# A cross network on one core: how the first block's chunk 2, tails and biases get to their places

## The chip, the core and the metric

The kernel runs on one core of a Trainium2 chip. The core has TensorE (PE; matmuls into PSUM, which has eight banks), VectorE (DVE), ScalarE (ACT), GpSimd (POOL), SyncE (SP, which here only issues DMAs), and 16 DMA engines that move data between HBM and SBUF. DMAs are issued on two queues here, SP's and ACT's. The metric is the device time of one execution in microseconds (us).

## The reference

```python
B, F, D, L = 4096, 26, 16, 6          # rows of 416 values, bfloat16
def reference(x0, ws, bs):            # x0 [4096, 416], ws [6, 416, 416], bs [6, 416]
    x = x0
    for l in range(ws.shape[0]):
        x = x0 * (x @ ws[l] + bs[l]) + x
    return x
```

## The kernel before, in words

The kernel never forms x. It keeps the sums x0 ws[0] + ... in PSUM: after layer l, PSUM holds the sum over layers of x @ ws, DVE adds a running sum of biases (plus one, from the ones row of `bsa_sb` and the triangle `u_sb`) and multiplies by x0. That gives the next x.

*Tiling.* The 4096 rows are worked in four pairs (p) of two blocks of 512 rows. Everything is transposed: features lie on partitions, rows of x0 in the free dimension. The 416 features are three chunks of 128 and a **tail** of 32. The tails of a pair are packed: four groups of 32 partitions hold the tails of the four quarters of 256 rows. A tail matmul therefore needs the 32 tail rows of the weights four times, at partitions 0, 32, 64 and 96 (`w3_sb`), and the tail-to-tail corner as a block diagonal 128 x 128 (`wc_sb`).

*Order on TensorE, written by hand.* For each of the 24 steps n = 6p + l: `main` for block 0 (helper `columns`, L398, L378), `tail` (L464: tail features into the chunks; then corners, L398; then chunks into the tail, L485), `main` for block 1. Step 0 is different: `first` (L345 on) takes the place of block 0's `main`.

*The start.* `idle` (L304) runs 28 matmuls of ones. SP's queue carries: half of x0's first 512 rows (`xin_sb`, 416 columns, L159), three chunks of ws[0] (L163), block 1 of x0 transposed by DMA (L166, three chunks), then, after the last chunk of ws[0] has landed, the weights of layers 1 to 5 (L171) each with its four tail copies (`four`, L174), and then the other pairs. ACT's queue carries the other half of `xin_sb` (L607), the tails of block 1 (`xtb_sb`, L610), the biases (`bsa_sb`, L613) and one copy of the tail weights of ws[0] (`w30_sb`, L614).

`first` turns the 512 rows on TensorE: 12 transposes (`turn`, L316), whose results DVE copies out in four pieces (L557). Then `biases` (L332, L338: three matmuls of 128 columns, and four of 32 into the four tail groups). Then, for each input chunk k of layer 0, four matmuls (helper `whole`, L388). After k = 0 come two transposes of the packed tails (L359), and `four_tails`: one matmul of `rep_sb` (four identities side by side) with `w30_sb`, which makes the four copies of the tail weights in PSUM.

DVE, after its four copies, takes the biases out (`cb_sb`, L562), then the tails (L567), and swaps halves of them (L570, semaphore s_dup). ACT takes the four tail copies out (L630) into `w3_sb`, then it and POOL copy two corners each into `wc_sb` (L623, L272). POOL packs the tails before that (L262), from `xin_sb` and `xtb_sb`. The first `tail` waits for the tails (s_ev, s_dup), the biases (s_cb), the weights (s_w30), and within it for the corners (s_wc0, s_wc) and for block 1 of x0 (s_x0[0]).

Of the kernel before, what the change touches and what calls it, by code (L numbers as in the profile page):

```python
# [11 lines left out]
def bass_standalone__dcn_v2_cross__recsys_kernel(  # L12
# [13 lines left out]
    B, D = x0.shape  # L26
# [13 lines left out]
    with ExitStack() as es:  # L40
# [7 lines left out]
        w30_sb = sb("w30_sb", [DR, D])  # L48
        rep_sb = sb("rep_sb", [DR, 128])
# [4 lines left out]
        xin_sb = sb("xin_sb", [128, 4, D])  # L54
        xtb_sb = sb("xtb_sb", [128, 4, DR])
# [13 lines left out]
        bsa_sb = sb("bsa_sb", [L + 1, D])  # L69
        u_sb = sb("u_sb", [L + 1, L])  # L70
# [22 lines left out]
        def blocks(l):  # L93

            gs = [slice(32 * g, 32 * g + 32) for g in range(4)]
            return [(wc_sb[g, l, g], w3_sb[g, l, DF:D]) for g in gs]
# [13 lines left out]
        s_bs, s_cb, s_wc = sem("s_bs"), sem("s_cb"), sem("s_wc")  # L110
        s_wt = [sem("s_wt%d" % i) for i in range(L)]
# [45 lines left out]
        def _(sp):  # L157

            sp.dma_start(  # L159
                xin_sb[:, 0:2, :], x0[0:256, :].rearrange("(j b) d -> b j d", b=128)  # L160
            ).then_inc(s_xin[0], 16)
            for k in range(3):
                sp.dma_start(  # L163
                    w_sb[:, 0, k, :], ws[0, k * 128:(k + 1) * 128, :]
                ).then_inc(s_w0[k], 16)
            sp.dma_start_transpose(  # L166
# [72 lines left out]
        def _(pool):  # L239
# [11 lines left out]
            pool.affine_select(  # L251
                out=rep_sb[:, :].rearrange("f (g e) -> f g e", e=DR),
                in_=ones_sb[0:DR, :].rearrange("f (g e) -> f g e", e=DR),
                pattern=[[0, 4], [-1, DR]], compare_op=ALU.is_equal, fill=0.0, base=0,
                channel_multiplier=1,
            ).then_inc(s_setup, 1)
            pool.memset(wc_sb[:, :, :], 0.0).then_inc(s_g, 1)

            for h, src in enumerate((xin_sb[:, :, DF:D], xtb_sb[:, :, :])):
                for x in (s_xin, (s_xtb,))[h]:  # L260
                    pool.wait_ge(x, 16)
                pool.tensor_copy(  # L262
                    out=xtn_sb[:, 0, :, :].rearrange(
                        "b c (h k f) -> b c h k f", h=2, f=DR
                    )[:, :, :, h, :],
                    in_=src.rearrange("b (h c) f -> b c h f", c=2),
                ).then_inc(s_xtp, 1)
            pool.wait_ge(s_xtp, 2)
            pool.wait_ge(s_g, 1)
            pool.wait_ge(s_w30, 1)  # L270
            for o, i in blocks(0)[2:]:
                pool.tensor_copy(out=o, in_=i).then_inc(s_wc0, 1)  # L272
            pool.wait_ge(s_wc0, 2)
# [25 lines left out]
        def _(pe):  # L299
# [6 lines left out]
            idle(28)  # L306
            pe.wait_ge(s_setup, 4)
            def at(c, j):

                return 4 if (c, j // 2) == (0, 1) else (2, 3, 6)[c]  # L310
# [13 lines left out]
            def four_tails():  # L324

                pe.wait_ge(s_wt[0], 16)
                whole(ps[:, 3, 0:D], rep_sb[:, :], w30_sb[:, :], True, True).then_inc(s_inT, 1)

            def biases():
                pe.wait_ge(s_bs, 16)  # L330
                for c in range(3):
                    pe.matmul(  # L332
                        ps[:, 7, D + c * 8:D + c * 8 + L],
                        lhsT=bsa_sb[:, c * 128:(c + 1) * 128], rhs=u_sb[:, :],
                        start=True, stop=True,
                    )
                for g in range(4):
                    ins = pe.matmul(  # L338
                        ps[32 * g:32 * g + 32, 7, D + 24:D + 24 + L],
                        lhsT=bsa_sb[:, DF:D], rhs=u_sb[:, :],  # L340
                        start=True, stop=True, tile_position=(0, 32 * g),
                    )
                ins.then_inc(s_inT, 1)

            def first():  # L345

                for c in range(3):
                    turn(c)
                biases()
                for k in range(3):  # L350
                    pe.wait_ge(s_w0[k], 16)
                    pe.wait_ge(s_ev, k + 2)
                    for m in range(3):
                        for o, x in pieces(0, m, xsrc(0, 0, 0, k)):
                            whole(o, w_sb[:, 0, k, m * 128:(m + 1) * 128], x, k == 0, False)
                    if k == 0:
                        pe.wait_ge(s_xtp, 2)
                        for c in range(2):
                            ins = pe.transpose(  # L359
                                out=psT[:, 2, c * 128:(c + 1) * 128],  # L360
                                in_=xtn_sb[:, 0, c, :], identity=ident[:, :],
                            )
                        ins.then_inc(s_inT, 1)
                        pe.wait_ge(s_ev, 3)
                        four_tails()
# [79 lines left out]
            def tail(p, l, n):  # L445
                if n == 0:
                    pe.wait_ge(s_ev, 5)
                    pe.wait_ge(s_cb, 1)
                    pe.wait_ge(s_w30, 1)
                elif l == 0:  # L450
                    pe.wait_ge(s_x0t[p], 16)
                elif n < L:
                    pe.wait_ge(s_wt[l], 16)
# [21 lines left out]
                if n == 0:  # L475
                    pe.wait_ge(s_wc0, 2)
                if n < L:
                    pe.wait_ge(s_wc, 4 * n + 2)
# [75 lines left out]
        def _(dve):  # L554
            for i, (c, j0, j1) in enumerate(((0, 0, 2), (0, 2, 4), (1, 0, 4), (2, 0, 4))):
# [3 lines left out]
                    in_=psT[:, (2, 4, 3, 6)[i], j0 * 128:j1 * 128],  # L559
                ).then_inc(s_ev, 1)  # L560
            dve.wait_ge(s_inT, 5)
# [4 lines left out]
            dve.wait_ge(s_inT, 6)  # L566
            dve.tensor_copy(out=x0t_sb[:, 0, 0, :], in_=psT[:, 2, 0:NT]).then_inc(s_ev, 1)  # L567
            dve.wait_ge(s_ev, 5)
            for o, i in swapped(x0t_sb[:, 0]):
                dve.tensor_copy(out=o, in_=i).then_inc(s_dup, 1)  # L570
# [35 lines left out]
        def _(act):  # L606
            act.dma_start(  # L607
                xin_sb[:, 2:4, :], x0[256:512, :].rearrange("(j b) d -> b j d", b=128)
            ).then_inc(s_xin[1], 16)
            act.dma_start(  # L610
                xtb_sb[:, :, :], x0[NB:2 * NB, DF:D].rearrange("(j b) d -> b j d", b=128)
            ).then_inc(s_xtb, 16)
            act.dma_start(bsa_sb[1:L + 1, :], bs[:, :]).then_inc(s_bs, 16)  # L613
            act.dma_start(w30_sb[:, :], ws[0, DF:D, :]).then_inc(s_wt[0], 16)  # L614
# [4 lines left out]
            def corner(l):  # L619
                if l > 0:  # L620
                    act.wait_ge(s_wt[l], 16)
                for o, i in blocks(l)[:2 if l == 0 else 4]:
                    act.activation(out=o, in_=i, func=ACTF.Copy).then_inc(s_wc, 1)  # L623

            def other(ap):
# [3 lines left out]
            act.wait_ge(s_inT, 7)  # L629
            act.activation(  # L630
                out=w3_sb[:, 0, :], in_=ps[:, 3, 0:D], func=ACTF.Copy
            ).then_inc(s_w30, 1)
            act.wait_ge(s_g, 1)
            act.wait_ge(s_w30, 1)
            corner(0)
# [79 lines left out]
```

## Time and profile before

| what | value |
| --- | --- |
| time, median of 3 runs | 129.96 us (129.71 to 130.29) |
| the profiled execution: time | 130.26 us |
| its span, first to last instruction | 128.5 us |
| TensorE busy | 124.4 us, 97% |
| DVE, ACT, POOL busy | 92.3, 45.9, 32.0 us |
| chain of waits that ended last | TensorE 97% |

The profile comes from one execution. A page of it gives the busy time of each engine, the chain of waits that ended last, groups of instructions by line (mean ns of one, idle time before them and what ended it), and DMA issues. Times within the span are counted from its start. "L388" is line 388 of the kernel before; helpers such as `whole` and `columns` carry the line for all that call them. A start of a matmul and the end of the one before it overlap, since they are pipelined. In the chain a piece begins where the piece before it ended. A DMA's "us to landing" is counted from the start of its issue.

### The profile page before, as it was taken

Reading aid. Unit: us, or ns where it says so; the run is one execution under the profiler, and the core shown is the slowest. Engines: PE = TensorE matmul, PEld = TensorE weight load, DVE = VectorE, ACT = ScalarE, POOL = GpSimd, SP = SyncE. Lnnn points to the kernel's source line nnn. Section 1 sums busy time; section 2 is a strip of 40 time slices with the busy share of each in tenths; the row PEclk is TensorE's granted clock in tenths of the full one; section 3 lists DMA queues with packets and bytes.
Section 4 is the critical chain, followed back from the end, with each engine's and each line's share of the span. In section 5 each row is a group of like instructions: output and inputs, shape, how many; then the busy total and the mean of one; then the engine's idle time right before and its main releaser. Section 6 shows DMA issues by size and latency. Waiting matters only on the chain.

```text
span 128.5 us, 5801 instructions
## 1 busy us (share of the span) xinstructions
PE 124.4 (97%) x2929; PEld 66.2 (52%) x2402; DVE 92.3 (72%) x152; ACT 45.9 (36%) x101; POOL 32.0 (25%) x40
## 2 busy tenths in 40 slices
PE   7999999999999999999999999999999999999990
PEld 7654554555445545545545545545545545546660
DVE  0439669669669669669679678688687697696482
ACT  1345446436404314314404224224214224225920
POOL 6123303303303203213113123123023033033050
PEclk9999999999999999999999999999999999999999
DMA  3979659665969940496300968000000857000026
GB/s 107 267 196 246 171 118 112 123 66 113 116 197 163 122 88 15 85 145 181 114 15 10 133 122 265 5 0 5 5 10 15 161 122 233 5 5 0 0 67 203
DMA packets 35463, 13.27 MB, mean 103 GB/s; under 512 B 26826, under 2 KB 35440, under 8 KB 35440
## 3 DMA queue, kind: packets, MB, share of 16 engines
q1 hardware_dynamic: 34436, 12.52, 48.7%
q10 hardware_dynamic: 1004, 0.38, 1.1%
q8 instruction: 21, 0.34, 1.1%
q14 instruction: 2, 0.02, 0.0%
HBM read 3.99 MB, written 3.41 MB: 58 GB/s over the span
## 4 chain that ended last, share of the span: by engine, by line
PE 97%; DVE 0%; issue 0%
PE ps L398 61%; PE ps L378 11%; PE ps L464 8%; PE ps L388 7%; PE ps L485 6%; PE ps L304 2%; PE ps L316 1%; DVE o_sb L600 0%; PE ps L528 0%; PE ps L332 0%; PE ps L338 0%; PE ps L359 0%
## 5 line engine op out<-in xcount | busy, mean ns | idle before, releaser
L579 DVE SCALAR_TENSOR_TENSOR xT_sb<-ps,cb_sb,x0T_sb 128x512 bf16<-128x512 f32 x100 | 69.3, 743 | 22.5 <-PE ps L464 22.5
L398 PE MATMUL ps<-xT_sb,w_sb 128*32 128x512 bf16 (+1 forms) x1380 | 75.7, 343 | 0.0
L398 PEld LDWEIGHTS ps<-xT_sb,w_sb 128*32 128x32 bf16 x1380 | 37.1, 97 | 35.0 <-issue 8.1
L285 POOL TENSOR_TENSOR xT_sb<-t_sb,x0T_sb 128x512 bf16<-128x512 f32 x20 | 23.3, 1163 | 72.0 <-ACT t_sb L661 72.0
L661 ACT ACTIVATE t_sb<-ps,cb_sb 128x512 f32<-128x512 f32 x23 | 15.8, 687 | 60.0 <-PE ps L464 60.0
L378 PE MATMUL ps<-xT_sb,w_sb 128*32 128x256 bf16 x444 | 26.6, 273 | 0.0
L627 ACT ACTIVATE xt_sb<-xt_sb 64x256 bf16<-64x256 bf16 x38 | 15.8, 415 | 9.8 <-DVE xt_sb L588 9.3
L398 PE MATMUL ps<-x0T_sb,w_sb 128*32 128x512 bf16 (+1 forms) x252 | 14.1, 344 | 0.0
L579 DVE SCALAR_TENSOR_TENSOR xo_sb<-ps,cb_sb,x0T_sb 128x512 bf16<-128x512 f32 x15 | 10.4, 743 | 3.3 <-PE ps L464 3.3
L398 PEld LDWEIGHTS ps<-x0T_sb,w_sb 128*32 128x32 bf16 x252 | 6.7, 97 | 6.5 <-issue 1.5
L464 PE MATMUL ps<-xt_sb,w_sb 32*128 32x256 bf16 x228 | 9.6, 271 | 0.0
L485 PE MATMUL ps<-xT_sb,w_sb 128*32 128x256 bf16 x228 | 9.5, 273 | 0.0
L588 DVE SCALAR_TENSOR_TENSOR xt_sb<-ps,cb_sb,x0t_sb 128x256 bf16<-128x256 f32 x20 | 9.5, 475 | 0.0
L464 PEld LDWEIGHTS ps<-xt_sb,w_sb 32*128 32x128 bf16 x228 | 4.2, 92 | 6.2 <-issue 6.1
L285 POOL TENSOR_TENSOR xo_sb<-t_sb,x0T_sb 128x512 bf16<-128x512 f32 x3 | 3.5, 1164 | 11.2 <-ACT t_sb L661 11.2
L485 PEld LDWEIGHTS ps<-xT_sb,w_sb 128*32 128x32 bf16 x228 | 6.1, 96 | 0.1
L398 PE MATMUL ps<-xt_sb,wc_sb 128*32 128x256 bf16 x76 | 5.6, 283 | 0.0
L623 ACT ACTIVATE wc_sb<-w_sb 32x32 bf16<-32x32 bf16 x22 | 5.0, 227 | 0.6
L388 PE MATMUL ps<-w_sb,xT_sb 128*128 128x416 bf16 x24 | 5.0, 339 | 0.0
L378 PE MATMUL ps<-x0T_sb,w_sb 128*32 128x256 bf16 x84 | 5.0, 273 | 0.0
L600 DVE SCALAR_TENSOR_TENSOR o_sb<-ps,xr_sb 128x416 bf16<-128x416 f32 x6 | 3.3, 585 | 2.4 <-PE ps L528 2.3
L557 DVE COPY x0T_sb<-ps 128x256 bf16<-128x256 bf16 (+1 forms) x4 | 1.4, 358 | 4.5 <-PE ps L316 4.3
(54 smaller groups left out, 48.3 us busy)
## 6 DMA issues: line engine op xcount, KB each, us to landing
out_dram<-o_sb SPq DMA_DIRECT2D x3, 832.0 KB, 4.9
w_sb<-in_ws_dram SPq DMA_DIRECT2D x5, 312.0 KB, 5.5
w_sb<-in_ws_dram SPq DMA_DIRECT2D x8, 104.0 KB, 3.4
xr_sb<-in_x_dram SPq DMA_DIRECT2D x1, 832.0 KB, 6.4
out_dram<-o_sb SPq DMA_DIRECT2D x3, 208.0 KB, 2.1
xin_sb<-in_x_dram SPq DMA_DIRECT2D x1, 208.0 KB, 3.0
xin_sb<-in_x_dram ACTq DMA_DIRECT2D x1, 208.0 KB, 3.3
x0T_sb<-in_x_dram SPq DMA_TRANSPOSE x13, 4.2
```

The lines of the kernel that those rows point to most:

```text
L285: pool.tensor_tensor(out=xdst(p, l, 0, 2), in0=t_sb[:, n % 2, :], in1=x0c(p, 0, 2), op=ALU.mult,).then_inc(s_pl, 1)
L378: return pe.add_instruction(mybir.InstMatmult(name="I-%d" % (1000000 + count[0]), engine=mybir.EngineType.PE, start_tensor_calc=start, sto ...
L388: return pe.matmul(out, lhsT=lhsT, rhs=rhs, start=start, stop=stop, skip_group_check=True)
L398: ins = pe.matmul(out[c:c + 32, :], lhsT=lhsT[:, c:c + 32], rhs=rhs, start=start, stop=stop, skip_group_check=True, tile_position=(0, c),)
L464: ins = pe.matmul(part(blk, m, h ^ other), lhsT=w3_sb[32 * g:32 * g + 32, l, m * 128:(m + 1) * 128], rhs=xt[32 * g:32 * g + 32, other, :], ...
L485: ins = pe.matmul(ps_tail[32 * g:32 * g + 32, :], lhsT=w_sb[:, l, k, DF:D], rhs=xsrc(p, l, g % 2, k)[:, (g // 2) * NT:(g // 2 + 1) * NT], ...
L579: dve.scalar_tensor_tensor(out=halves(xdst(p, l, blk, c)), in0=chunk2(blk, c), scalar=cb_sb[:, c, l:l + 1], in1=halves(x0c(p, blk, c)), op ...
L588: dve.scalar_tensor_tensor(out=tdst(p, l), in0=ps_tail, scalar=cb_sb[:, 3, l:l + 1], in1=x0t_sb[:, p, 0, :], op0=ALU.add, op1=ALU.mult,).t ...
L600: dve.scalar_tensor_tensor(out=o_sb[:, (NP - 1) * TT + j, :], in0=ps[:, BANK[j], 0:D], scalar=1.0, in1=xr_sb[:, j, :], op0=ALU.add, op1=AL ...
L623: act.activation(out=o, in_=i, func=ACTF.Copy).then_inc(s_wc, 1)
L627: act.activation(out=o, in_=i, func=ACTF.Copy).then_inc(s_dup, 1)
L661: act.activation(out=halves(t_sb[:, n % 2, :]), in_=chunk2(0, 2), func=ACTF.Identity, bias=cb_sb[:, 2, l:l + 1],).then_inc(s_act, 1)
```

## The change

Block 0's chunk 2 is no longer turned on TensorE: `xin_sb` holds 256 columns, and a DMA transpose on SP's queue, ahead of that of block 1, brings chunk 2. The third chunk of ws[0] moves to ACT's queue. The tails of both blocks come in one load (`xtb_sb`, 1024 rows of 32 values) on ACT's queue. The tail weights of ws[0] come as two copies in one load (`two`) straight into the lower half of `w3_sb`, and ACT copies that half to the upper; `four_tails`, `rep_sb` and `w30_sb` are gone. The four corners of layer 0 are all copied by POOL, one after the other, straight from the loaded rows. The biases are issued last on ACT's queue; POOL makes four copies of their tail part (`bs4_sb`), so that four equal matmuls make the sums; those stand after k = 1 now. The last chunk, k = 2, waits for the DMA transpose in place of a DVE copy. There are 27 idle matmuls. DVE takes the biases out after the tails.

```diff
-        w30_sb = sb("w30_sb", [DR, D])
-        rep_sb = sb("rep_sb", [DR, 128])
...
-        xin_sb = sb("xin_sb", [128, 4, D])
-        xtb_sb = sb("xtb_sb", [128, 4, DR])
+        xin_sb = sb("xin_sb", [128, 4, 256])
+        xtb_sb = sb("xtb_sb", [128, TT, DR])
...
+        bs4_sb = sb("bs4_sb", [L + 1, 4, DR])
...
+        def two(l):
+            return ws[l, DF:D, :].unsqueeze(0).broadcast_to([2, DR, D])
...
         def _(sp):
             sp.dma_start(
-                xin_sb[:, 0:2, :], x0[0:256, :].rearrange("(j b) d -> b j d", b=128)
+                xin_sb[:, 0:2, :], x0[0:256, 0:256].rearrange("(j b) d -> b j d", b=128)
             ).then_inc(s_xin[0], 16)
-            for k in range(3):
+            for k in range(2):
                 sp.dma_start(
                     w_sb[:, 0, k, :], ws[0, k * 128:(k + 1) * 128, :]
                 ).then_inc(s_w0[k], 16)
+            sp.dma_start_transpose(
+                out=x0T_sb[:, 2, 0:NB], in_=x0[0:NB, 256:DF]
+            ).then_inc(s_xa2, 16)
             sp.dma_start_transpose(
                 out=x0T_sb[:, :, NB:2 * NB], in_=x0[NB:2 * NB, 0:DF]
             ).then_inc(s_x0[0], 16)
...
         def _(pool):
...
-            for h, src in enumerate((xin_sb[:, :, DF:D], xtb_sb[:, :, :])):
-                for x in (s_xin, (s_xtb,))[h]:
-                    pool.wait_ge(x, 16)
+            pool.wait_ge(s_xtb, 16)
+            for k in range(2):
                 pool.tensor_copy(
...
-            pool.wait_ge(s_w30, 1)
-            for o, i in blocks(0)[2:]:
-                pool.tensor_copy(out=o, in_=i).then_inc(s_wc0, 1)
-            pool.wait_ge(s_wc0, 2)
+            pool.wait_ge(s_bs, 16)
+            pool.wait_ge(s_setup, 1)
+            pool.tensor_copy(
+                out=bs4_sb[:, :, :], in_=bsa_sb[:, DF:D].unsqueeze(1).broadcast_to([L + 1, 4, DR])
+            ).then_inc(s_bs4, 1)
+            pool.wait_ge(s_g, 1)
+            pool.wait_ge(s_wt[0], 16)
+            for g in range(4):
+                gs = slice(32 * g, 32 * g + 32)
+                pool.tensor_copy(out=wc_sb[gs, 0, gs], in_=w3_sb[0:DR, 0, DF:D]).then_inc(s_wc0, 1)
+                pool.wait_ge(s_wc0, g + 1)
...
         def _(pe):
-            idle(28)
-            pe.wait_ge(s_setup, 4)
+            idle(27)
+            pe.wait_ge(s_setup, 3)
...
-            def four_tails():
-
-                pe.wait_ge(s_wt[0], 16)
-                whole(ps[:, 3, 0:D], rep_sb[:, :], w30_sb[:, :], True, True).then_inc(s_inT, 1)
-
             def biases():
-                pe.wait_ge(s_bs, 16)
-                for c in range(3):
-                    pe.matmul(
+                pe.wait_ge(s_bs4, 1)
+                for c in range(4):
+                    ins = pe.matmul(
                         ps[:, 7, D + c * 8:D + c * 8 + L],
-                        lhsT=bsa_sb[:, c * 128:(c + 1) * 128], rhs=u_sb[:, :],
-                        start=True, stop=True,
-                    )
-                for g in range(4):
-                    ins = pe.matmul(
-                        ps[32 * g:32 * g + 32, 7, D + 24:D + 24 + L],
-                        lhsT=bsa_sb[:, DF:D], rhs=u_sb[:, :],
-                        start=True, stop=True, tile_position=(0, 32 * g),
+                        lhsT=bsa_sb[:, c * 128:(c + 1) * 128] if c < 3
+                        else bs4_sb[:, :, :].rearrange("l g f -> l (g f)"),
+                        rhs=u_sb[:, :], start=True, stop=True,
                     )
                 ins.then_inc(s_inT, 1)
 
             def first():
 
-                for c in range(3):
+                for c in range(2):
                     turn(c)
-                biases()
                 for k in range(3):
                     pe.wait_ge(s_w0[k], 16)
-                    pe.wait_ge(s_ev, k + 2)
+                    if k < 2:
+                        pe.wait_ge(s_ev, k + 2)
+                    else:
+                        pe.wait_ge(s_xa2, 16)
...
                         ins.then_inc(s_inT, 1)
-                        pe.wait_ge(s_ev, 3)
-                        four_tails()
+                    elif k == 1:
+                        biases()
...
                 if n == 0:
-                    pe.wait_ge(s_ev, 5)
+                    pe.wait_ge(s_ev, 4)
                     pe.wait_ge(s_cb, 1)
                     pe.wait_ge(s_w30, 1)
+                    pe.wait_ge(s_wt[0], 16)
...
         def _(act):
             act.dma_start(
-                xin_sb[:, 2:4, :], x0[256:512, :].rearrange("(j b) d -> b j d", b=128)
+                xin_sb[:, 2:4, :], x0[256:512, 0:256].rearrange("(j b) d -> b j d", b=128)
             ).then_inc(s_xin[1], 16)
             act.dma_start(
-                xtb_sb[:, :, :], x0[NB:2 * NB, DF:D].rearrange("(j b) d -> b j d", b=128)
+                xtb_sb[:, :, :], x0[0:2 * NB, DF:D].rearrange("(j b) d -> b j d", b=128)
             ).then_inc(s_xtb, 16)
+            act.dma_start(w_sb[:, 0, 2, :], ws[0, 256:DF, :]).then_inc(s_w0[2], 16)
+            act.dma_start(w3_sb[0:64, 0, :], two(0)).then_inc(s_wt[0], 16)
             act.dma_start(bsa_sb[1:L + 1, :], bs[:, :]).then_inc(s_bs, 16)
-            act.dma_start(w30_sb[:, :], ws[0, DF:D, :]).then_inc(s_wt[0], 16)
...
-            act.wait_ge(s_inT, 7)
+            act.wait_ge(s_wt[0], 16)
             act.activation(
-                out=w3_sb[:, 0, :], in_=ps[:, 3, 0:D], func=ACTF.Copy
+                out=w3_sb[64:128, 0, :], in_=w3_sb[0:64, 0, :], func=ACTF.Copy
             ).then_inc(s_w30, 1)
-            act.wait_ge(s_g, 1)
-            act.wait_ge(s_w30, 1)
-            corner(0)
```

## The prediction

> **What bounds the kernel now.** I read the page first. TensorE is busy nearly the whole span and the chain that ended last is made of it:
>
> ```profile
> PE 124.4 (97%) x2929; PEld 66.2 (52%) x2402; DVE 92.3 (72%) x152; ACT 45.9 (36%) x101; POOL 32.0 (25%) x40
> ...
> PE 97%; DVE 0%; issue 0%
> ```
>
> So from the first tail matmul of layer 0 (L464) on, TensorE waits for nothing. The change touches only what comes before that point; later work can absorb no delay and return no gain. The question is when that first L464 matmul starts. The chain of waits over the first microseconds (start, length, what) says when it does now:
>
> ```profile
> 3.97 1.40 PE ps L316 x12
> 5.37 0.17 PE ps L332 x3
> 5.54 0.12 PE ps L338 x2
> 5.66 1.13 PE ps L388 x4
> 6.79 0.11 PE ps L359 x2
> 6.90 0.28 PE ps L388
> 7.18 0.16 issue
> 7.34 1.25 PE ps L388 x7
> 8.59 0.44 PE ps L464 x12
> ```
>
> The tail starts at **8.59**. Note the speed: four matmuls (1536 columns) take 1.13 us at 5.66, and twice that takes 1.25 at 7.34; twelve turns take 1.40, but two take 0.11 at 6.79. TensorE runs at half speed until about 6.4. Third, the stretches by window (last two columns: DMA busy share, GB/s):
>
> ```profile
> 2.00:6.00 4.00, 4.00 (x40) 3.23 (x38) 1.44 (x5) 1.49 (x2) 1.37 (x4) 1.00 1.11 278
> 6.00:6.50 0.50, 0.50 (x3) 0.23 (x2) 0.00 (x0) 0.00 (x0) 0.00 (x0) 1.00 0.72 155
> 5.50:6.00 0.50, 0.50 (x8) 0.21 (x7) 0.42 (x2) 0.00 (x0) 0.00 (x0) 1.00 1.27 289
> 7.75:8.00 0.25, 0.25 (x4) 0.12 (x3) 0.00 (x0) 0.17 (x1) 0.11 (x1) 1.00 1.09 369
> 8.25:8.50 0.25, 0.25 (x3) 0.05 (x1) 0.00 (x0) 0.06 (x1) 0.16 (x2) 1.00 0.86 77
> 8.50:8.75 0.25, 0.25 (x10) 0.22 (x12) 0.00 (x0) 0.00 (x0) 0.18 (x1) 1.00 0.76 70
> 26.50:27.00 0.50, 0.50 (x16) 0.28 (x12) 0.50 (x2) 0.26 (x2) 0.00 (x0) 1.00 0.31 29
> ```
>
> The DMA engines are full from 2.0 to about 6.3. From 7.75 to 8.00 a plain layer load flows (832-byte rows, 369 GB/s). Then, although the layer-2 load was issued at 6.96, the rate falls to 70 to 77: what flows is the tail load of layer 1 (`four`, L174), four copies of 32 rows. An engine moving such rows does 369/16 = 23 GB/s, so it uses about three to four of the 16, and holds back what is queued behind it.
>
> **TensorE's own work.** One idle matmul less is 0.11, but now the first turn also waits for x0's rows until 3.8 (issue 0.79 + 3.0 to landing). They shrink from 416 to 256 columns, so I let the turns start at 3.75: 0.2 gained. Eight turns instead of twelve end at 4.65 (0.107 each). The first layer matmuls wait for the second DVE copy: 4.86 now, at best 4.75 then. k=0 at half speed: 1.28 (twice the 0.64 of a full-speed one), to 6.05; two tail turns, 0.22, to 6.27; k=1 0.7, to **7.0**. The `rep_sb` matmul and the gap behind it (0.28 + 0.16) are gone. Then come the biases, four matmuls, 0.2, and k=2, 0.64. With nothing late the tail would start at 7.8, a gain of 0.77.
>
> **What must be there by then.**
> - *Chunk 2 by DMA.* Issued at 2.27. Its issue is bounded by 1.24 (the L189 transpose) and 1.58 (L166, three chunks). Its 131 KB take 0.45 at 289 GB/s, up to 0.9 shared, and 0.5 more to landing: about 5.3, at most 6.5 (by the 4.2 of L166). Wanted at 7.2 or later: nothing, hidden by k=0 and k=1. Copying chunk 2 on DVE (0.42) goes and nothing waited for it.
> - *Small tails.* 1024 pieces of 64 bytes instead of 512: 65 KB at 29/0.31 = 94 GB/s, 0.70 instead of 0.35, landing about 4.9; two POOL copies (0.29 each) end at 5.5, wanted at 6.05. Nothing.
> - *x0 block 1* (L166) is pushed behind chunk 2: issue 3.55 to 5.14, needed in the tail's third part, 0.66 after the tail starts. See below.
> - *Layer 1 and later weights.* SP is free at 5.14 instead of 5.76, and w0's third chunk now comes on ACT's queue; they are issued at 5.2 to 5.6 and needed at 11.4. Nothing.
> - *Setup and queues.* The select that made `rep_sb` (0.30 on POOL, done at 2.1) goes; the first turn is at 3.75: nothing. ACT issues five loads instead of four, so its table load ends near 5 instead of 4.2; ACT's next work waits for the tail weights: nothing. DVE's bias copy is moved behind the three tail copies, which end at 7.4; it waits for the biases anyway.
> - *Tail weights and biases* are what I think decides. The load `two` is of the same kind as `four`: two copies of 32 rows of 832 bytes. The biases (6 rows) are moved **behind** it on ACT's queue, and the bias matmuls now stand **ahead of k=2**, so TensorE's queue stops there until the biases land and POOL has copied four tails of them.
>
> **When they land.** In full-rate terms all DMA ahead of `two` on its engines is: x0 262 KB, 0.85 (between 0.71 at 369 and the present 1.15); w0 0.87; small tails 0.70; chunk 2 0.45: 2.87. The present load sums to 1.15 + 0.87 + 0.35 + 0.09 + 1.36 = 3.82 the same way and took 4.3, so I scale by 1.13: `two` starts at 4.9 to 5.25. If it runs on two engines it takes 53 KB at 46 GB/s, 1.15, or 1.4 to 1.5 at half of the 70 to 77 seen. Block 1's transposes (1.36) are ready at 5.14 on the other queue. Alone `two` ends at 6.1 to 6.4; shared evenly, at 7.2 to 7.8. Even sharing is what the trace shows: the two halves of x0, issued within 0.01 on two queues, landed 3.0 and 3.3 after issue. With 0.5 to landing (the transposes' share falls at 6.4, L166 lands at 2.75 + 4.2), weights and biases are there at T = 6.6 to 8.3. I take **T = 7.7**, near the shared end.
>
> The Trainium skill, page DMA: Bandwidth & Descriptors, section "Rules for kernel authors", says that the slowest dimension sets the number of DMA engines and that "a leading zero-stride broadcast of c copies — confines the whole DMA to at most c engines". The rate of the four-copy load agrees (70 to 77 of 369 GB/s). It speaks against this change: by it `two` has two engines; were it spread over 16, it would cost 0.15.
>
> **From T to the tail.** POOL starts 0.05 after the landing (small tails: 1.31 + 3.4 = 4.71, copy at 4.73). The bias copy, 7 x 128, is in no row: between 0.18 (L247, 7 x 6) and 0.29 (L262, 128 x 128); I take 0.25. To TensorE 0.15 (the gap at 7.18), biases 0.2, k=2 0.64: tail at T + 1.29, so **break-even is T = 7.3**. With 7.7 it starts at 8.99: **+0.40**. TensorE idles from 7.0 to about 8.15. The other inputs of the tail fit beside this: ACT's copy of 64 x 416, bounded by the rows below, ends at T + 0.7; DVE's bias copy (0.17) at T + 0.95; POOL's four corners, now one after the other, 0.24 to 0.35 each, I take 0.28, end at T + 1.5, wanted at T + 1.73. Block 1 on the loaded engines: 2.0 + 1.13 (2.87 + 1.15 + 1.36) = 8.1, landing 8.6, wanted at 9.6.
>
> ```profile
> 7.22 0.52 ACT L630 ACTIVATE w_sb<-ps 128x416 bf16<-128x416 f32 x1 [2.83 <-PE ps L388]
> 7.83 0.48 ACT L623 ACTIVATE wc_sb<-w_sb 32x32 bf16<-32x32 bf16 x2
> 7.89 0.47 POOL L272 COPY wc_sb<-w_sb 32x32 bf16<-32x32 bf16 x2 [2.87 <-ACT w_sb L630]
> ```
>
> These are the chain now: TensorE makes four copies, ACT takes them out (0.52), ACT and POOL split the corners. It is short because the 32 rows land at 2.53 + 3.2 = 5.73.
>
> **Sum.** The profiled execution took 130.26 (span 128.5, 1.76 around it), 0.30 above the median of the runs, 129.96. 130.26 + 0.40 = **130.7**. I do not take off the 0.30: the new start hangs on a DMA. Half a per cent (0.65) is about what a measurement of this kernel can tell from no change.
>
> **Rivals.**
> - *Forecast: late biases.* T of 7.2 to 8.2: 130.2 to 131.1. Chance 0.60; above 130.61 (T over 7.65) 0.36 of it, within half a per cent 0.24.
> - *Faster: the load is quick.* If `two` is served ahead of the transposes or spread over more engines, T is below 6.8, the biases are found ready or nearly so, and the shorter TensorE work shows: tail 7.8 to 8.1, 129.5 to 129.8 on the profiled run; TensorE then sets the pace as it does now, so the median's 0.30 comes off: 129.2 to 129.5. It gains from T = 7.3 down. For it: `two` and the transposes are on different queues. Against: four copies at 70 to 77 GB/s. Chance 0.20, of it 0.07 below 129.31.
> - *Later still.* The transposes go first: `two` starts after 5.25 + 1.5 and ends at 8.3, T = 8.8, tail 10.1: 131.8. For it: a stalled load held back the layer-2 load at 8.25. Chance 0.13.
> - *Half speed again.* The stall of 1.2 us brings back the half speed that lasted from 0.83 to 6.4. If it comes back for between the stall's length and those 5.6 us, half of it is lost on top: 0.6 to 2.8, so 131.3 to 133.5. Against: no row shows it after 6.4. Chance 0.04. The Trainium skill, page TensorE: Matmul & The Clock Gate, section "What's actually happening", gives free windows of about 3.4 us, an idle one of which brings half speed back; by that one window is an estimated 1.7, and a stall of 1.2 does not fill one. The trace agrees in the start only.
> - *Nothing:* the edits cancel, 130.3. Chance 0.03.
>
> Faster 0.07; same 0.24 + 0.13 + 0.03 = 0.40; slower 0.36 + 0.13 + 0.04 = 0.53. The range 129.4 to 131.4 leaves out 0.09 of the quick case, 0.07 of the late one and the 0.04: 0.20.
>
> **What would show it.** Right: TensorE idle between k=1 and the bias matmuls, ended by POOL's bias copy, which waited for the bias DMA; the first L464 matmul near 9.0; the two tail-weight loads landing after 7. Turns starting at 3.75, k=1 ended near 7.0, and no wait for chunk 2, each test a step. Wrong: biases landing by 6.5, the tail waiting for something else (corners, block 1, DVE's bias copy), or a TensorE difference after the first tail.

## The result and the profile after

The kernel after took **130.83 us** (130.63 to 131.00, five runs) beside 129.87 for the kernel before on the same chip (129.58 to 130.29, five runs): ratio 1.0066 [1.0044, 1.0088], so slower by about two thirds of a per cent. The profiled execution took 130.63, its span is 128.8. The page again shows a kernel that TensorE sets, but the chain that ended last is no longer made of TensorE alone:

```profile
PE 123.3 (96%) x2921; PEld 65.5 (51%) x2393; DVE 92.0 (71%) x151; ACT 45.5 (35%) x99; POOL 32.3 (25%) x42
...
PE 92%; issue 4%; POOL 2%; DVE 0%; POOLq 0%
```

TensorE's busy time fell by 1.1 us (124.4 before; a part of this is that, by the clock that the trace records, it ran at full speed from 4.85 on, and before from 6.39), and the kernel got slower all the same. The chain of waits over the first microseconds (start, length, what) shows why:

```profile
5.22 2.26 issue
7.48 0.02 POOLq L270
7.50 0.00 issue
7.50 0.29 POOL bs_sb L266
7.79 0.05 issue
7.84 0.25 PE ps L328 x4
8.09 0.76 PE ps L381 x4
8.85 0.44 PE ps L458 x12
9.28 0.22 PE ps L391 x4
9.51 0.33 PE ps L479 x12
```

The first tail matmul (L458, before: L464) starts at 8.85, where it started at 8.59. Ahead of it stand k=2 (L381), the bias matmuls (L328) and POOL's copy of the bias tails (L266). The "issue" of 2.26 us is POOL with nothing to do. The view of waits names what it and TensorE wait for (total, times, longest):

```profile
POOL bs_sb L266 <- DMA bsa_sb<-in_bs_dram: 2.3, 1, 2.3
...
PE ps L328 <- POOL bs_sb L266: 1.5, 1, 1.5
```

TensorE had ended k=1 at 6.36 and stood still for 1.5 us. What became of the steps that made the tail weights before (a matmul, a copy of 0.52 by ACT, corners by ACT and POOL) is in the timeline:

```profile
7.08 0.55 ACT L629 ACTIVATE w_sb<-w_sb 64x416 bf16<-64x416 bf16 x1 [1.61 <-DMA w_sb<-in_ws_dram]
...
7.50 0.28 POOL L266 COPY bs_sb<-bsa_sb 7x128 bf16<-7x128 bf16 x1 [2.28 <-DMA bsa_sb<-in_bs_dram]
7.74 0.99 POOL L273 COPY wc_sb<-w_sb 32x32 bf16<-32x32 bf16 x4
```

The tail weights landed at 7.05, and in the trace the last of the biases at 7.45. The stretches show what the DMA engines did then (last two columns: DMA busy share, GB/s):

```profile
6.00:6.25 0.25, 0.25 (x3) 0.08 (x1) 0.22 (x2) 0.00 (x0) 0.00 (x0) 1.00 1.37 88
6.25:6.50 0.25, 0.11 (x2) 0.00 (x0) 0.22 (x2) 0.00 (x0) 0.00 (x0) 1.00 0.47 87
6.50:6.75 0.25, 0.00 (x0) 0.00 (x0) 0.05 (x1) 0.00 (x0) 0.00 (x0) 1.00 0.37 47
...
7.00:7.25 0.25, 0.00 (x0) 0.00 (x0) 0.00 (x0) 0.17 (x1) 0.00 (x0) 1.00 1.28 291
```

From 6.0 to 6.75 they move 47 to 88 GB/s, although block 1's transposes had been issued from 3.52 to 5.23; these flow at 291 only from 7.0. In the packets of the trace, the 64 rows of `two` pass from 5.1 to 6.45, 14 in each 0.25 us; the transposes move 40 to 130 pieces in each 0.25 us until 7.0 and 284 after it.

One more reading places the runs below, but for those in which block 1 itself is late (6 and 11). From the first tail matmul to the end of the span it is 119.9 us before (128.5 - 8.59) and 120.0 after (128.8 - 8.85). So the span is the start of the first tail plus 120.0, and nothing after it changed.

### The profile page after: what moved, and what is told of

Same layout as the page of the kernel before. It is cut to its first block, busy times and chain, and to the rows that moved or that the text cites. A ratio compares the mean times of both kernels' runs of the same rounds, so it can differ in the third digit from the quotient of the medians.

```text
span 128.8 us, 5781 instructions
## 1 busy us (share of the span) xinstructions
PE 123.3 (96%) x2921; PEld 65.5 (51%) x2393; DVE 92.0 (71%) x151; ACT 45.5 (35%) x99; POOL 32.3 (25%) x42
## 4 chain that ended last, share of the span: by engine, by line
PE 92%; issue 4%; POOL 2%; DVE 0%; POOLq 0%
PE ps L391 61%; PE ps L371 11%; PE ps L458 8%; PE ps L479 6%; PE ps L381 5%; POOL wc_sb L253 1%; DVE o_sb L594 0%; PE ps L522 0%; POOL xtn_sb L257 0%; POOL bsa_sb L243 0%; POOL bs_sb L266 0%; POOL ident L245 0%; PE ps L328 0%; POOL ones_sb L242 0%; POOL u_sb L249 0%
## 5 line engine op out<-in xcount | busy, mean ns | idle before, releaser
L391 PE MATMUL ps<-xT_sb,w_sb 128*32 128x512 bf16 (+1 forms) x1380 | 75.7, 343 | 0.0
L391 PEld LDWEIGHTS ps<-xT_sb,w_sb 128*32 128x32 bf16 x1380 | 37.0, 97 | 35.1 <-issue 8.1
L391 PE MATMUL ps<-x0T_sb,w_sb 128*32 128x512 bf16 (+1 forms) x252 | 14.1, 343 | 0.0
L391 PEld LDWEIGHTS ps<-x0T_sb,w_sb 128*32 128x32 bf16 x252 | 6.8, 97 | 6.4 <-issue 1.5
L458 PE MATMUL ps<-xt_sb,w_sb 32*128 32x256 bf16 x228 | 9.6, 271 | 0.0
L458 PEld LDWEIGHTS ps<-xt_sb,w_sb 32*128 32x128 bf16 x228 | 4.2, 92 | 6.2 <-issue 6.1
L391 PE MATMUL ps<-xt_sb,wc_sb 128*32 128x256 bf16 x76 | 5.6, 283 | 0.0
L381 PE MATMUL ps<-w_sb,xT_sb 128*128 128x416 bf16 x24 | 5.0, 339 | 0.0
L619 ACT ACTIVATE wc_sb<-w_sb 32x32 bf16<-32x32 bf16 x20 | 4.5, 226 | 0.5
L391 PEld LDWEIGHTS ps<-xt_sb,wc_sb 128*32 128x32 bf16 x76 | 1.9, 92 | 4.0 <-issue 4.0
```

Of the source, the lines that this page charges most:

```text
L381: return pe.matmul(out, lhsT=lhsT, rhs=rhs, start=start, stop=stop, skip_group_check=True)
L391: ins = pe.matmul(out[c:c + 32, :], lhsT=lhsT[:, c:c + 32], rhs=rhs, start=start, stop=stop, skip_group_check=True, tile_position=(0, c),)
L458: ins = pe.matmul(part(blk, m, h ^ other), lhsT=w3_sb[32 * g:32 * g + 32, l, m * 128:(m + 1) * 128], rhs=xt[32 * g:32 * g + 32, other, :], ...
L619: act.activation(out=wc_sb[gs, l, gs], in_=w3_sb[gs, l, DF:D], func=ACTF.Copy).then_inc(s_wc, 1)
```

## Experiments

The theories, as the expectations name them. **A**, the forecast's: the two-copy load passes its 64 rows through two engines, and so holds up the biases behind it and the transposes. **B**: only the biases are late, by their place in the queue. **C**: there is simply too much DMA in this stretch. **D**: not DMA, but the new order on TensorE and POOL's chain of copies. Later ones: **F**: whatever load or completion falls into the time of the transposes is late, and transposes move on all engines together, at the pace of the busiest. **G**: the chunk-2 transpose is late by itself. **H**: the small tails, 1024 pieces now, are what makes the loads late.

In the table, "tail" is the start of the first tail matmul in the profiled execution; ratios are to the kernel before, run beside each. The start is taken from the chain, for kernel 11, whose chain does not pass it, from the timeline. The profiled execution of the first, the third and the fourth was the longest of all their runs (131.0, 130.72 and 130.94): their traces are read for what waits for what, not for the time.

| kernel | median us (range) | ratio | tail | span |
| --- | --- | --- | --- | --- |
| after | 130.83 (130.63-131.00) | 1.0066 [1.0044, 1.0088] | 8.85 | 128.8 |
| 1 biases first | 130.19 (129.86-131.00) | 1.0029 [1.0009, 1.0050] | 9.24 | 129.3 |
| 2 two loads | 130.32 (130.13-130.54) | 1.0031 [1.0019, 1.0043] | 8.47 | 128.4 |
| 3 both | 130.20 (129.78-130.72) | 1.0017 [0.9998, 1.0036] | 8.88 | 128.9 |
| 4 four copies | 130.71 (130.57-130.94) | 1.0066 [1.0046, 1.0085] | 9.11 | 129.1 |
| 5 bias matmuls after k=2 | 130.69 (130.63-131.15) | 1.0063 [1.0040, 1.0086] | 8.90 | 128.9 |
| 9 small loads first | 131.06 (130.66-132.49) | 1.0117 [1.0072, 1.0162] | 9.24 | 129.2 |
| 10 chunk 2 on TensorE | 130.17 (129.87-130.76) | 1.0016 [0.9999, 1.0033] | 8.44 | 128.5 |
| 11 block 1 after ws[0]'s second chunk | 130.29 (130.01-130.52) | 1.0018 [0.9999, 1.0038] | 7.95 | 128.4 |
| 12 block 1 after ws[0]'s first chunk | 129.72 (129.47-130.26) | 0.9984 [0.9967, 1.0002] | 7.86 | 127.9 |

### 1. The biases issued ahead of the two-copy load

```diff
-            act.dma_start(w3_sb[0:64, 0, :], two(0)).then_inc(s_wt[0], 16)
             act.dma_start(bsa_sb[1:L + 1, :], bs[:, :]).then_inc(s_bs, 16)
+            act.dma_start(w3_sb[0:64, 0, :], two(0)).then_inc(s_wt[0], 16)
```

> One edit to the changed kernel: the bias load is issued ahead of the two-copy tail load on ACT's queue. Theory A (the 64 rows of the two-copy load pass through two DMA engines, from about 5.1 to 6.45, and hold back what shares those engines: the biases behind them and the DMA transposes beside them): the biases land by 5.6 and the bias matmuls follow k=1 at once, but chunk 2 still lands near 7.25, so the stall moves to k=2; first tail matmul near 8.0 instead of 8.78; time 129.9 to 130.3. Rival B (the biases alone are late; chunk 2 has time to spare): no stall is left, tail at 7.2 to 7.7, time 129.3 to 129.7. Rival C (all DMA of the start is late because there is too much of it): biases still after 6.5, time above 130.4.

Measured 130.19: the ratio falls from 1.0066 to 1.0029, so more than half of the loss is gone by a swap of two lines. The swap also has the biases issued earlier, at 2.48 in place of 3.63, since ACT took 1.11 to issue the two-copy load. The biases landed at 5.60, and their matmuls followed k=1 at once. Then the next inputs were late. k=2 waited 0.9 for the chunk-2 transpose (landed 7.76), and the tail for the weights, in the chain of waits:

```profile
3.35 5.11 DMA w_sb<-in_ws_dram
8.46 0.02 issue
8.49 0.56 ACT w_sb L629
9.04 0.20 issue
9.24 0.51 PE ps L458 x12
```

So B names the first wait rightly, but the biases were only the first of three that were held up.

### 2. Two loads of 32 rows in place of one of two copies

```diff
-            act.dma_start(w3_sb[0:64, 0, :], two(0)).then_inc(s_wt[0], 16)
+            for h in range(2):
+                act.dma_start(
+                    w3_sb[32 * h:32 * h + 32, 0, :], ws[0, DF:D, :]
+                ).then_inc(s_wt[0], 16)
...
-            act.wait_ge(s_wt[0], 16)
+            act.wait_ge(s_wt[0], 32)
```

(POOL's and TensorE's waits for s_wt[0] become 32 too.)

> One edit to the changed kernel: the two copies of the tail rows come by two loads of 32 rows each in place of one load with a leading dimension of two; same rows, same bytes, same place in ACT's queue. Theory A: spread over the engines the rows take some 0.15, the weights land by 6, chunk 2 by 5.8, the biases by 6.1; first tail matmul at 7.2 to 7.9, by where the half speed of TensorE ends; time 129.1 to 129.7, faster than both kernels. Rival C (too much DMA in all: 1024 small pieces, a transpose more): landings as in the changed kernel within 0.3, time 130.4 to 130.9. Rival D (the order on TensorE and POOL's bias copy cost the time): tail not before 8.4 although the loads land early, time above 130.3.

A miss: 130.32, about 0.5 better than after, where 1.1 to 1.7 was expected. The same bytes on all engines still landed late: chunk 2 at 6.67, weights at 6.94, biases at 7.07. The chain is that of after, moved by 0.38:

```profile
7.12 0.29 POOL bs_sb L266
7.42 0.05 issue
7.46 0.25 PE ps L328 x4
7.71 0.16 issue
7.87 0.60 PE ps L381 x3
8.47 0.44 PE ps L458 x12
```

### 3. Both edits together

```diff
-            act.dma_start(w3_sb[0:64, 0, :], two(0)).then_inc(s_wt[0], 16)
             act.dma_start(bsa_sb[1:L + 1, :], bs[:, :]).then_inc(s_bs, 16)
+            for h in range(2):
+                act.dma_start(
+                    w3_sb[32 * h:32 * h + 32, 0, :], ws[0, DF:D, :]
+                ).then_inc(s_wt[0], 16)
```

> Both edits together: two loads of 32 rows, and the biases issued ahead of them. Theory A: as with two loads alone, within 0.2: with the rows spread nothing is late behind them, so the order of the two loads is worth nothing; time 129.1 to 129.7. Rival B (the biases' place is what counts): better than two loads alone by 0.3 or more. Rival C: no better than the bias load ahead alone.

A miss again: 130.20, no better than the first alone. The biases landed at 5.72, but the weights, now last in the queue, at 8.11 in its trace, though its 64 rows were spread over all engines. A alone does not explain this; something else still holds the last load.

### 4. All four copies by one load, without ACT's copy

```diff
-            act.dma_start(w3_sb[0:64, 0, :], two(0)).then_inc(s_wt[0], 16)
+            act.dma_start(w3_sb[:, 0, :], four(0)).then_inc(s_wt[0], 16)
...
-            act.wait_ge(s_wt[0], 16)
-            act.activation(
-                out=w3_sb[64:128, 0, :], in_=w3_sb[0:64, 0, :], func=ACTF.Copy
-            ).then_inc(s_w30, 1)
```

> One edit to the changed kernel: the tail rows come as four copies in one load (as in the other layers), and ACT's copy to the upper half goes: twice the bytes. Theory A: 32 rows per engine as before, on four engines instead of two, so the rows flow at twice the rate over the same 1.3 us; weights near 7.1, biases near 7.4, time within 0.2 of the changed kernel's 130.83. Rival C (bytes count): 53 KB more on queues that are full come 0.15 to 1.3 later; time 131.0 to 132.0.

130.71: twice the bytes over twice the outer dimension cost the same. The landings moved by a quarter of a microsecond only (weights 7.31, biases 7.71, chunk 2 7.52). If the bytes set the time (C), 53 KB more would have shown.

### 5. The bias matmuls after k=2

```diff
-                    elif k == 1:
+                    elif k == 2:
                         biases()
```

> One edit to the changed kernel: the bias matmuls stand behind k=2. If chunk 2 were hidden with time to spare, as predicted before the change was run (landing 5.3), k=2 would fill the stall at once and end before the biases' copy. Theory F, by the landings seen (chunk 2 at 7.25, biases at 7.45): TensorE still waits from k=1 to 7.3, now for chunk 2, and the tail, which needs the biases through DVE, starts some 0.2 to 0.3 earlier than before: time 130.4 to 130.7. Rival B' (the bias matmuls' place ahead of k=2 is what costs): the whole 0.65 of k=2 is won, time 130.0 to 130.25.

130.69, as expected: the order of the matmuls is not what costs (against D; POOL's copies, the other half of D, stay in kernel 12, which is level with before). k=2 meets a wait of its own, for the transpose that the forecast had landed by 5.3 and at most 6.5:

```profile
2.27 5.18 DMA x0T_sb<-in_x_dram
7.45 0.14 issue
7.59 0.81 PE ps L381 x4
8.40 0.18 PE ps L328 x4
8.58 0.32 issue
8.90 0.51 PE ps L458 x12
```

### 6. Block 1's transposes held until the biases have landed

```diff
+            sp.wait_ge(s_bs, 16)
             sp.dma_start_transpose(
                 out=x0T_sb[:, :, NB:2 * NB], in_=x0[NB:2 * NB, 0:DF]
```

> The changed kernel, but SP issues the transposes of block 1 (and all behind them) only when the biases have landed. Theory F: without them the two-copy load has its engines to itself: chunk 2 lands at 5.2 to 5.8 instead of 7.25, weights by 6.7, biases by 6.9; then block 1 lands after 9.5 and the tail's third part waits for it: time 131.0 to 132.0. Rival G' (chunk 2 is late because of the two-copy load alone): chunk 2 still near 7.

One execution: 132.82. Its time is that of the new wait: block 1 landed at 11.57 and the tail's third part (L480 in this run) started at 11.62. Its landings are what it is for. With no other transposes in the way, 14 engines had delivered chunk 2 by 6.42; the other two, at 7.34 and 7.73. The biases, on six engines, landed at 6.51 to 6.57 on four and at 7.52 and 7.91 on two; the two-copy load landed at 7.17 and 7.55. The trace does not name a packet's engine, but the pairs follow one another at the same distance (7.17, 7.34, 7.52 and 7.55, 7.73, 7.91). So the two-copy load delays chunk 2 on what must be the engines that carry it, by 0.9 to 1.3 us, with the rest of SP's queue empty.

### 7. and 8. The load alone, in the kernel before

To the kernel before, a load of the same 64 rows is added at the end of ACT's queue, into a buffer that nothing reads; what is computed does not change. Once as one load of two copies, once as two loads of 32 rows.

```diff
+            act.dma_start(
+                scr_sb[:, :], ws[0, DF:D, :].unsqueeze(0).broadcast_to([2, DR, D])
+            ).then_inc(s_scr, 16)
```

> The kernel before with one more load, last on ACT's queue: the two-copy load of the tail rows into a buffer that nothing reads. Theory F: its 32 rows on each of two engines hold back block 1's transposes on all engines from about 4.8 to 6.2, so that block 1 lands at 7.6 to 8.4 instead of 6.97; nothing waits for that before 9.1, so the time stays within 0.4 of 129.9. Rival (an engine's queue delays only its own share, and shares are interleaved): block 1 lands by 7.3, and in the stretch from 5 to 6 the rate stays at 218 to 289 GB/s.

```diff
+            for h in range(2):
+                act.dma_start(
+                    scr_sb[32 * h:32 * h + 32, :], ws[0, DF:D, :]
+                ).then_inc(s_scr, 16)
```

> The same, the unread copies by two loads of 32 rows each: the same bytes over all engines, four rows on each. Theory F: 0.15 of work on each engine, so block 1 lands at 7.0 to 7.3; time within 0.4 of 129.9. Rival (the amount counts, not the shape): as with the one load.

One execution each: 132.16 against **130.28**, beside 129.95 for the kernel before (129.52 to 130.47, eleven runs); so the second cannot be told from no change. The size of the first was a miss (within 0.4 was expected), and the mechanism stronger than thought. A load that nobody waits for, behind all others of its queue, delays block 1 of x0 on the *other* queue: landed at 10.42, 6.97 without it. The third chunk of ws[0], also on SP's queue, lands at 7.20 in place of 5.75, and the biases, ahead of it on its own queue, at 5.77 in place of 4.93. With two loads block 1 lands at 7.97 (at most 7.3 was expected).

Not all of the 2.2 us is DMA. Block 1 still came before the tail's third part (11.10), so its delay cost nothing here. TensorE waited 0.5 for the biases, and by the recorded clock it ran at half speed until 9.82, where the kernel before did until 6.39:

```profile
6.17 1.39 PE ps L391 x4
7.56 0.21 PE ps L362 x2
7.77 0.45 PE ps L391
...
8.56 1.88 PE ps L391 x7
10.44 0.44 PE ps L467 x12
```

The first tail is 1.85 later than before. The same matmuls (L391 here, L388 before, and the two tail turns) take 3.93 in place of 2.77, so 1.2 of the 1.85 is half speed. Whether the wait for the biases put off the step to full speed, one execution does not show.

The stretches of the first (where the kernel before had 289 GB/s):

```profile
7.00:7.50 0.50, 0.50 (x5) 0.38 (x3) 0.00 (x0) 0.00 (x0) 0.00 (x0) 1.00 1.27 100
7.50:8.00 0.50, 0.50 (x4) 0.10 (x2) 0.19 (x1) 0.00 (x0) 0.00 (x0) 1.00 1.28 99
```

and of the second:

```profile
6.00:6.50 0.50, 0.50 (x4) 0.31 (x3) 0.00 (x0) 0.00 (x0) 0.00 (x0) 1.00 1.31 281
```

The busy share is the same (1.27 to 1.31) and the rate a third: an engine whose piece waits counts as busy, so the GB/s have to be read. The packets say what the pace is. From 6.75 to 7.75 the first has 5 rows of the extra load in each 0.25 us and 77 to 82 pieces of the transposes, 5 for each of the 16 engines. The transposes move one piece per engine for each row that the loaded engine reads: as if all 16 moved together. On the loaded engine row and piece seem to alternate: an estimate from 369/16 GB/s for a row and 290/16 for a piece is 0.036 + 0.014 = 0.050 us for one of each, and the rows start 0.05 apart. The rows do not explain all of it: from 4.75 to 6.25, before the load's first row (6.35), the transposes moved 46 to 115 pieces in each 0.25 us, where the kernel before had 182 to 284, and what held them there is open. Plain rows are not held in this way: from 8.75 to 9.5, beside 3 to 7 rows of the load, 74 to 91 rows of layer 1's weights pass in each 0.25 us. The rule that the prediction cites (the Trainium skill, page DMA: Bandwidth & Descriptors, section "Rules for kernel authors") says how few engines serve such a load, and the trace agrees (5 rows of 832 bytes per 0.25 us, 17 GB/s, from one engine after the other). That the engines without it slow down as well is what the trace adds.

### 9. Biases and weights ahead of the small tails

The biases and the two loads of 32 rows are issued before the small tails and the third chunk of ws[0], on the same queue.

```diff
+            act.dma_start(bsa_sb[1:L + 1, :], bs[:, :]).then_inc(s_bs, 16)
+            for h in range(2):
+                act.dma_start(
+                    w3_sb[32 * h:32 * h + 32, 0, :], ws[0, DF:D, :]
+                ).then_inc(s_wt[0], 16)
             act.dma_start(
                 xtb_sb[:, :, :], x0[0:2 * NB, DF:D].rearrange("(j b) d -> b j d", b=128)
```

> The changed kernel with the biases and the tail weights (two loads of 32 rows) issued on ACT's queue right behind its half of x0, ahead of the small tails and of the third chunk of ws[0]. Theory F (the runs so far: what counts is not the shape of the tail load alone; any load whose rows or completion fall into the time of the DMA transposes is late, because a transfer's transposes advance on all engines together at the pace of the busiest one, and completions wait for them): weights and biases land by 5.0, no wait for biases, tail matmuls start at 7.2 to 7.9, time 129.1 to 129.7. Rival G (chunk 2's transpose is late by itself, because a second transpose follows it at once): chunk 2 still lands after 6.5 and k=2 waits for it; tail 7.4 to 8.1, time 129.6 to 130.0.

A miss: 131.06, no better than after. What was put first came in time (biases 3.71, weights 5.59), and what was put last was late instead: small tails 6.74 (4.65 in after), ws[0]'s third chunk 6.98. The loads of this queue cannot be sorted so that none is late.

### 10. Chunk 2 on TensorE again

Kernel 3, with `xin_sb` at 384 columns, 12 turns, four DVE copies and no chunk-2 transpose.

```diff
-            sp.dma_start_transpose(
-                out=x0T_sb[:, 2, 0:NB], in_=x0[0:NB, 256:DF]
-            ).then_inc(s_xa2, 16)
...
-                for c in range(2):
+                for c in range(3):
                     turn(c)
```

> The kernel with both edits, and chunk 2 of block 0 turned on TensorE and copied by DVE as in the kernel before (x0's rows loaded with 384 columns); the other parts of the change stay. TensorE gets four turns more at half speed, 0.43, and k=2 no longer waits for a DMA. Theory F: one transfer of transposes is left; biases and weights land by 6.3; tail at 8.0 to 8.3, time 129.5 to 129.9. Rival H (the small tails as 1024 pieces are what makes the loads late): landings as in the kernel with both edits, 6.7 and later, time 130.1 to 130.6.

130.17, the same as kernel 3: a miss, and it speaks against G. Without that DMA the weights still landed at 7.66, and ACT's copy of them (to 8.23) ends the wait. This is what rival H expected (130.1 to 130.6); kernels 11 and 12 speak against H, since they keep the small tails and have the weights at 6.42 and 6.82. What remains on SP's queue at that time is block 1.

### 11. and 12. Block 1's transposes held for a short while

Kernel 3, with SP waiting for the second or for the first chunk of ws[0] before it issues block 1's transposes.

```diff
+            sp.wait_ge(s_w0[1], 16)
             sp.dma_start_transpose(
                 out=x0T_sb[:, :, NB:2 * NB], in_=x0[NB:2 * NB, 0:DF]
```

> The kernel with both edits (two loads of 32 rows, biases ahead of them), and SP issues block 1's transposes only when the second chunk of ws[0] has landed (about 5.0). Theory F: chunk 2 lands by 5.9, biases by 5.6, weights by 6.2, since only chunk 2's transposes share the engines with them; the tail starts at 7.2 to 7.9; block 1, issued at 5.0 to 6.6, lands by 8.6 and is wanted 0.66 after the tail's start, so at most 0.3 is lost there; time 129.2 to 129.7, below both kernels. Rival G (chunk 2's transpose is late by itself): chunk 2 after 6.5, time 129.8 to 130.3.

```diff
+            sp.wait_ge(s_w0[0], 16)
             sp.dma_start_transpose(
                 out=x0T_sb[:, :, NB:2 * NB], in_=x0[NB:2 * NB, 0:DF]
```

> The kernel with both edits, and SP issues block 1's transposes when the first chunk of ws[0] has landed (about 4.2 instead of 3.5 unasked, or 5.0 with the wait for the second chunk). Theory F: their packets start near 5.6, when the tail weights' rows are read, so weights and biases land by 6.5 as with the later wait, and block 1 lands by 8.2 instead of 8.8: no wait for it; time 129.6 to 130.0, 0.3 to 0.6 below the version that waits for the second chunk. Rival G (transposes that follow another transfer of transposes are slow at any time): weights or chunk 2 after 6.5, time 130.0 to 130.4.

With the later wait every small load comes early (biases 5.85, chunk 2 6.04, weights 6.42), TensorE has no stall through k=2, and the first tail starts at 7.95. The time is still 130.29, a miss: block 1 is now the late one.

```profile
5.04 3.77 DMA x0T_sb<-in_x_dram
8.81 0.04 issue
8.85 0.51 PE ps L480 x12
```

L480 is the tail's third part, due at 8.6. With the earlier wait (issued at 4.4 in place of 5.04) block 1 lands at 8.31, and the chain has no gap from the tail turns on:

```profile
5.98 0.28 PE ps L353 x2
6.27 0.65 PE ps L382 x4
6.92 0.18 PE ps L329 x4
7.10 0.76 PE ps L382 x4
7.86 0.44 PE ps L459 x12
8.29 0.22 PE ps L392 x4
8.52 0.35 PE ps L480 x12
```

**129.72** (twelve runs) beside 129.99 (eighteen runs of before): ratio 0.9984 [0.9967, 1.0002], within the 129.6 to 130.0 expected. That is about 1.1 us below after; against the kernel before it is no gain that can be told from none. In its trace the small tails landed at 5.35, and the tail turns waited 0.5 us for POOL's copies of them; that is the next late input.

## Why the prediction was right, point by point

It was right in the sign, the size and the place: 130.7 was forecast and 130.83 measured, and TensorE's stall is ended by POOL's bias copy, which waited for the biases behind `two`. How the biases came to be late was only in part foreseen, and the closeness of the number is in part luck, as the fourth point says. By its steps:

- *TensorE's own work.* Turns from 3.66 (3.75 forecast), k=0 from 4.77 (4.75). k=1 ended at 6.36, not 7.0: full speed came at 4.85 in this execution and at 6.39 in that of before, so k=0 ran at full speed. It made the stall longer (1.5, not 1.15) and the time no better.
- *Landing of weights and biases.* T = 7.7 forecast, in 6.6 to 8.3; 7.05 and 7.45 measured. So the break-even of 7.3 was passed, by 0.15. Kernel 1 shows the step by undoing it: with the biases at 5.60 the time is 0.6 lower.
- *From T to the tail.* 1.29 forecast, 1.40 measured: 0.05 to POOL, 0.28 (0.25), 0.06 to TensorE (0.15), 0.25 (0.2), 0.76 (0.64). POOL's corners, at a pitch of 0.26, ACT's copy (0.55) and DVE's bias copy (8.31) were hidden, as said; block 1 landed at 8.41 (8.6 said).
- ***Even sharing* failed.** `two` was not slowed by the transposes: its rows passed at 14 per 0.25 us, 47 GB/s, which is what the two engines were said to give alone. The transposes gave way. That took it to 6.45, and 0.6 more to landing (0.5 said). By the forecast's own 0.5 from the last row to the landing, the biases would have been there at 6.95, ahead of the break-even. They came at 7.45 by a wait that the forecast did not have: the increments of four of their six engines were in the trace's packets from 5.10 to 5.22 and landed at 7.17 to 7.23; the other two landed at 7.44 and 7.45. So T came out within 0.25 because one error (a load quicker than shared) was made up by another (later completions).
- ***Chunk 2 by DMA, "about 5.3, at most 6.5 ... hidden by k=0 and k=1"*, failed.** It landed at 7.25 in after: three engines by 5.75, thirteen from 6.90 on. It cost nothing here only because the biases came later still, and it decides in kernel 5 (7.45) and in part in kernel 1. The upper bound was taken from a row, 4.2 from issue to landing, in which no load on few engines ran beside the transposes; kernel 7 shows that such a load takes that same row to 7.7.
- *The base.* The forecast kept the profiled execution's 130.26 and did not take off the 0.30 to the median, since the new start hangs on a DMA. That was the right choice. The spans of after are 128.8 to 129.2, in the middle 129.0, so by the 120.0 above its usual first tail is at 9.0 (8.99 forecast). The executions of before beside these runs have spans from 127.8, in the middle 128.2: its usual first tail is near 8.2, and the profile's 8.59 was a late one. So the change costs an estimated 0.8 in the usual execution (0.96 by the medians), although the two profiles differ by 0.26 only.
- *The rivals.* The quick load did not come (in kernel 2, where the load is spread, the weights land at 6.94 and the gain is 0.5 only). "Transposes first" has the two queues the wrong way round. Half speed did not come back: after the idle 1.5 us the four matmuls of k=2 take 0.82 from first start to end, k=1 took 0.81. "Nothing" is excluded by the interval of the ratio.

What the runs show of the loss (0.66% in after): put the biases first and 0.29% is left (1); spread the load and 0.31% is (2); both together leave 0.17% (3), which the intervals do not tell from either alone. Issue block 1's transposes 0.9 us later as well, and the kernel is level with before (12; the intervals of 3 and 12 only just touch). So two things make up the loss: the load's shape and its place ahead of the biases, and transposes issued into the time of the small loads. Whether the second cure alone would do, with the two-copy load kept, was not tried; kernel 6 holds block 1 far too long to tell.

What stays open: why completions wait for transposes when no load of many rows on few engines is about (in kernels 2, 3 and 10 the weights land at 6.94, 8.11 and 7.66). In after, four of the engines that carry the biases had read their rows by about 5.2, and reported them at 7.17 to 7.23. The Trainium skill, page DMA: Bandwidth & Descriptors, section "Queues, rings and completion order", says that the increment of a semaphore "lands only after every earlier write from that SDMA engine, across its queues". The trace agrees, as 5.2 and 7.17 beside transposes that end at 7.25 show, and kernels 11 and 12 agree: with block 1 issued later, the weights land at 6.42 and 6.82, where kernel 3 has them at 8.11. That it is the writes of the transposes, and not their reads, was not measured.

## What to carry to other kernels

Ask of each load not only its bytes, but over how many engines it goes and what else those engines carry: a load of 53 KB that nothing waits for took the landing of another queue's transposes from 6.97 to 10.42 as one broadcast of two copies, and to 7.97 as two plain loads (one execution each). When a step is moved to DMA, bound its landing by rows in which the same company was on the engines; a duration from a quiet stretch is no upper bound. When one late input is cured, compute the next in line before counting on the gain: here biases, chunk 2, weights and block 1 landed within 1.4 us of each other, and three of the cures (2, 3 and 11) paid about half of what was expected or less.

## What the runs showed of the hardware that was not expected

- Transposes by DMA on SP's queue fell from 284 pieces per 0.25 us to 77 to 82 while one engine read 5 rows per 0.25 us for ACT's queue (kernel 7). It is not strict: in kernel 6 fourteen engines were done 0.9 to 1.3 us ahead of the loaded two.
- The two queues do not share by time. In after, from 3.50 to 3.75, 554 pieces of 64 bytes (the small tails, ACT's queue) passed, and one row of 832 bytes of SP's.
- The step to full speed of TensorE came at 4.85 in the profiled execution of after and at 6.39 in that of before; over all the profiled executions it lies between 3.49 (kernel 2) and 9.82 (kernel 7). In kernel 7 it moved the first tail by 1.2 us, more than any change here is worth; one profile of the start does not compare two kernels.
